# A gated-MLP kernel on one Trainium2 core: the low three bits of each weight made on ScalarE, and two weight subtractions on VectorE

## The chip, the core and the metric

The program runs on one NeuronCore of a Trainium2 chip. The core has five instruction engines, each with a queue of its own that it works off in order: TensorE (PE in the profile; its weight loads are PEld), VectorE (DVE), ScalarE (ACT), GpSimd (POOL) and SyncE (SP), which here only issues DMAs. An instruction that waits for another engine holds up everything behind it in its own queue. The metric is the device time of one execution in microseconds (us), from several timed runs. A profiled execution gives the trace; its span runs from the first to the last instruction.

## The reference, cut to what matters

An mLSTM attention over 768 steps feeds two MLPs. The arithmetic wanted is that of float32, and the weights arrive as float64.

```python
C = f_stab * C + i_stab * einsum('bhd,bhe->bhde', vt, kt)      # 768 steps, 2 x 8 heads, head size 40
n = f_stab * n + i_stab * kt
y[t] = sigmoid(o_gate[t]) * (C @ qt) / maximum(abs(n @ qt), 1)
x = y as 1536 tokens x 320
x = ((x @ w_a) * (x @ w_b)) @ w_out                            # hidden size 1536
h = x @ w_in                                                   # hidden size 2048
return (h * sigmoid(h)) @ w_out2                               # 1536 x 320
```

## The kernel before

**Attention.** The 768 steps are cut into 6 chunks of 128 for each of 2 batches: 12 units, u0 to u11. For a unit, TensorE makes the scores (L348), VectorE builds a matrix of decay factors by a running scan (L328, 128x1024) and multiplies the scores by it (L355), TensorE forms the values (L361) and the carried part (L371) and updates the state (L381), and VectorE and GpSimd finish the unit (L419 to L435). The unit is then transposed on TensorE (`px`, L451) and stored as a high and a low part in a ring of six slots (`xring`).

**MLPs.** Products are kept near float32 by splitting every factor into a high part that the fast matmul format holds and a low part, the rest after subtracting the high part. `first_layer` (L472, tile `h`) multiplies a block of two or three units by the 128 hidden columns of tile j; the first MLP does it twice, ScalarE copies one result (`a`, L505) and VectorE multiplies the two into `g` (L511). In the second MLP ScalarE applies Silu instead (L516). `split_g` splits `g`: ScalarE casts the high part (L487) and GpSimd subtracts (L196). `second_layer` (L481 to L483) accumulates into `acc`. The first MLP has 12 weight tiles, the second 16.

**Weight preparation.** Each weight is a float64, seen as two 32-bit words: `raw[..., 0]` is the low word, `raw[..., 1]` the high word. `narrowed` builds the float32 `c` (tiles `cvt`): ScalarE scales the high word so that its bits, shifted left by three, are those of the float32 (L189); VectorE shifts left by three (L190) and then takes the top three bits of the low word and ORs them in (L191). After it, ScalarE casts the high part into the weight tile `w_j`, and the subtraction `rest` (L196, a helper with one line for all callers) makes the low part. In the first MLP a weight tile comes in two pieces: part 0 of 512 elements per partition ("w3.a" in the order list), part 1 of 448 ("w3.b"). Of part 1 the first 128 columns are handled in two halves of 64 partitions: ScalarE casts a half (L213), GpSimd subtracts into a small tile `tl`, and a DMA on SP carries it to the other 64 partitions of `w_j` (L215). In the second MLP a tile is one piece of 704.

**Order.** A list written out by hand (`ORDER`) names all attention, weight and MLP steps up to the last block of the first MLP; a scheduler then places each engine's instructions by that list, by priorities and by its own estimate of when each is ready. So a changed instruction can move others. Buffers: four `raw` tiles for the first MLP and three for the second, two `cvt` tiles of each size.

The two narrow places of the code that the text needs are these, where `eng` chooses the engine of a subtraction:

```python
def rest(eng, out_, x, hi):
    return eng.tensor_tensor(out=out_, in0=x, in1=hi.bitcast(F32), op=ALU.subtract)
```

Of the kernel before, what the change touches and what calls it, by code (L numbers as in the profile page):

```python
# [8 lines left out]
F32 = mybir.dt.float32  # L9
F32R = mybir.dt.float32r  # L10
BF16 = mybir.dt.bfloat16
U32 = mybir.dt.uint32

# [51 lines left out]
ACT = mybir.ActivationFunctionType  # L67
ALU = mybir.AluOpType
# [3 lines left out]
def tile_mlstm_gated_mlps(ctx: ExitStack, tc: tile.TileContext, i_gate, f_gate, q_cols, k_cols, kvo, w1, w2,  # L72
                          out):
    nc = tc.nc
# [3 lines left out]
    P = 128  # L78
# [87 lines left out]
    raw = {}  # L166
    w1_32, w2_32 = (w.bitcast(U32).rearrange("j p (f t) -> j p f t", t=2) for w in (w1, w2))

    def load_w1(j):
        parts_ = []  # L170
        for f in (slice(0, 4 * P), slice(4 * P, 5 * P + DM)):
            t = raws.tile([P, f.stop - f.start, 2], U32, tag="raw", name=f"raw1_j{j}")
            nc.sync.dma_start(out=t, in_=w1_32[j, :, f])
# [3 lines left out]
    def load_w2(j):  # L177
        t = wp2.tile([P, 3 * P + DM, 2], U32, tag="raw2", name=f"raw2_j{j}", bufs=3)
        nc.sync.dma_start(out=t, in_=w2_32[j])
        raw[2, j] = t  # L180
# [2 lines left out]
    W = {}  # L183

    def narrowed(r, c):
        lo32, hi32 = r[:, :, 0], r[:, :, 1]
        cu = c.bitcast(U32)

        nc.scalar.activation(out=c, in_=hi32.bitcast(F32), func=ACT.Prelu, scale=2.0 ** -111, alpha=-2.0 ** 32)  # L189
        nc.vector.tensor_scalar(out=cu, in0=cu, scalar1=3, scalar2=None, op0=ALU.logical_shift_left)  # L190
        nc.vector.scalar_tensor_tensor(out=cu, in0=lo32, scalar=29, in1=cu,  # L191
                                       op0=ALU.logical_shift_right, op1=ALU.bitwise_or)
        return c

    def rest(eng, out_, x, hi):
        return eng.tensor_tensor(out=out_, in0=x, in1=hi.bitcast(F32), op=ALU.subtract)  # L196


    def split_w1(j, part):
        if (1, j) not in W:  # L200
            W[1, j] = wp.tile([P, WN], F32R, tag="w", name=f"w1_j{j}", bufs=J1)
        t, r = W[1, j], raw[1, j][part]
        if part == 0:
            c = narrowed(r, cvt.tile([P, 4 * P], F32, tag="cvt", name=f"cvt_j{j}"))
            nc.scalar.copy(out=t[:, 0:4 * P], in_=c)
            rest(nc.gpsimd, t[:, 6 * P:10 * P], c, t[:, 0:4 * P])
            return
        c = narrowed(r, cvt.tile([P, P + DM], F32, tag="cvt", name=f"cvt_j{j}"))
        tl = cvt.tile([P, P], F32R, tag="tl", name=f"tl_j{j}")
        for n in range(2):  # L210
            p, q_ = slice(n * KT, (n + 1) * KT), slice((1 - n) * KT, (2 - n) * KT)
            s_ = slice((4 + n) * P, (5 + n) * P)
            nc.scalar.copy(out=t[p, s_], in_=c[p, 0:P])  # L213
            rest(nc.gpsimd, tl[p], c[p, 0:P], t[p, s_])
            nc.sync.dma_start(out=t[q_, s_].bitcast(F32), in_=tl[p].bitcast(F32))  # L215
        nc.scalar.copy(out=t[:, 10 * P:10 * P + DM], in_=c[:, P:])
        rest(nc.gpsimd, t[:, 10 * P + DM:], c[:, P:], t[:, 10 * P:10 * P + DM])


    def split_w2(j, pool, tag, bufs):  # L220
        r = raw.pop((2, j))
        t = pool.tile([P, 5 * P + 2 * DM], F32R, tag=tag, name=f"w2_j{j}", bufs=bufs)
        c = narrowed(r, wp2.tile([P, 3 * P + DM], F32, tag="cvt2", name=f"cvt2_j{j}", bufs=2))
        nc.scalar.copy(out=t[:, 0:3 * P], in_=c[:, 0:3 * P])  # L224
        rest(nc.gpsimd, t[:, 3 * P:5 * P], c[:, 0:2 * P], t[:, 0:2 * P])
        rest(nc.gpsimd, t[KT:P, 2 * P:3 * P], c[KT:P, 2 * P:3 * P], t[KT:P, 2 * P:3 * P])
        nc.scalar.copy(out=t[:, 5 * P:5 * P + DM], in_=c[:, 3 * P:])
        rest(nc.gpsimd, t[:, 5 * P + DM:], c[:, 3 * P:], t[:, 5 * P:5 * P + DM])
        W[2, j] = t
# [358 lines left out]
    for j in range(J1):  # L588
        parts[f"lw{j}"] = lambda j=j: load_w1(j)
        parts[f"w{j}.b"] = lambda j=j: split_w1(j, 1)  # L590
        parts[f"w{j}.a"] = lambda j=j: split_w1(j, 0)
# [7 lines left out]
    for t in ORDER:  # L599
        n = t.lstrip("!")  # L600
# [112 lines left out]
```

## Time and profile before

| | us |
|---|---|
| timed runs, median of three (lowest, highest) | 496.28 (493.99, 496.87) |
| the profiled execution's own time | 493.73 |
| its span | 491.8 |
| TensorE busy | 468.7 |
| TensorE weight loads busy | 460.8 |
| GpSimd busy | 261.5 |
| ScalarE busy | 210.6 |
| VectorE busy | 199.8 |

Shares over the whole span say little here: weights are prepared in the first quarter and again around the middle, attention ends near the middle, and the last third is matmuls alone. So the profile is read by stretches of time. "Idle before, releaser" in a row is time in which the engine had nothing running, and what ended it. Matmul rows show overlapping instructions, so a mean of 300 ns does not say that one leaves every 300 ns.

### The profile page before, as it was taken

How to read it: one execution, taken by the hardware profiler on the slowest of the kernel's cores; microseconds unless marked ns; L12 is line 12 of the kernel's file. 1: busy time of each engine (PE TensorE's matmuls, PEld its weight loads, DVE VectorE, ACT ScalarE, POOL GpSimd, SP SyncE). 2: the span in 40 equal slices, each digit the busy share in tenths (PEclk: the TensorE clock that was granted, in tenths of full speed). 3: DMA queues.
4: the chain of work that ended last, by engine and by line, in shares of the span. 5: the costliest groups of instructions: out<-in, count | busy, mean ns of one | idle time of the engine just before them, and what ended most of it. 6: DMA issues, size and time to landing. Idle time of an engine off the chain costs nothing.

```text
span 491.8 us, 8440 instructions
## 1 busy us (share of the span) xinstructions
PE 468.7 (95%) x3261; PEld 460.8 (94%) x3261; DVE 199.8 (41%) x328; ACT 210.6 (43%) x479; POOL 261.5 (53%) x305
## 2 busy tenths in 40 slices
PE   7999887799999999999999999999999999999996
PEld 6988887798999999999999998899999999999996
DVE  7988989978533346523741555400100010000000
ACT  4347655563222331222645554833433453334332
POOL 5569998898432332322853877853433333343332
PEclk9888998899999999999999999999999999999999
DMA  7786857734210012105550343000010000001001
GB/s 228 218 255 205 262 174 215 210 109 131 88 55 1 14 59 58 42 1 176 176 177 1 123 171 119 0 1 1 1 41 0 1 21 21 1 0 41 1 0 40
DMA packets 25090, 42.32 MB, mean 86 GB/s; under 512 B 2156, under 2 KB 18348, under 8 KB 25052
## 3 DMA queue, kind: packets, MB, share of 16 engines
q1 hardware_dynamic: 25052, 41.80, 27.0%
q8 instruction: 25, 0.41, 0.4%
q14 instruction: 13, 0.11, 0.1%
HBM read 38.99 MB, written 2.02 MB: 83 GB/s over the span
## 4 chain that ended last, share of the span: by engine, by line
PE 67%; POOL 11%; DVE 8%; DMA 4%; issue 4%; ACT 4%; SPq 1%; ACTq 0%; POOLq 0%; DVEq 0%
PE h L472 35%; PE acc L481 8%; PE acc L483 8%; PE acc L482 8%; POOL w_j L196 7%; PE s_u L348 3%; PE y_u L361 2%; ACT cvt_j L189 2%; POOL g L196 2%; DVE e_u L328 2%; DMA raw_j<-in_w_dram 2%; DVE cvt_j L191 1%; DVE cvt_j L190 1%; PE px_u L451 1%; PE y_u L371 1%
## 5 line engine op out<-in xcount | busy, mean ns | idle before, releaser
L472 PE MATMUL h<-xring,w_j 128*128 128x384 f32 (+1 forms) x1472 | 260.3, 319 | 6.6 <-DVE g L511 4.2
L472 PEld LDWEIGHTS h<-xring,w_j 128*128 128x128 f32 x1472 | 229.9, 190 | 9.1 <-DVE g L511 5.1
L196 POOL TENSOR_TENSOR g<-g,g 128x384 fp32r<-128x384 f32 (+1 forms) x124 | 119.1, 961 | 185.5 <-ACT g L487 184.5
L487 ACT CAST g<-g 128x384 fp32r<-128x384 f32 (+1 forms) x124 | 59.8, 482 | 110.4 <-DVE g L511 71.8
L481 PE MATMUL acc<-w_j,g 128*128 128x320 f32 x336 | 102.4, 314 | 0.6 <-ACT g L487 0.6
L482 PE MATMUL acc<-w_j,g 128*128 128x320 f32 x336 | 101.0, 309 | 0.0
L483 PE MATMUL acc<-w_j,g 128*128 128x320 f32 x336 | 77.0, 313 | 1.2 <-POOL g L196 1.2
L196 POOL TENSOR_TENSOR w_j<-cvt_j,w_j 128x320 fp32r<-128x320 f32 (+2 forms) x72 | 69.7, 969 | 6.5 <-ACT w_j L224 3.0
L481 PEld LDWEIGHTS acc<-w_j,g 128*128 128x128 f32 x336 | 63.5, 189 | 1.4 <-ACT g L487 1.2
L482 PEld LDWEIGHTS acc<-w_j,g 128*128 128x128 f32 x336 | 63.5, 189 | 0.0
L483 PEld LDWEIGHTS acc<-w_j,g 128*128 128x128 f32 x336 | 56.7, 188 | 2.4 <-POOL g L196 2.4
L516 ACT ACTIVATE g<-h 128x384 f32<-128x384 f32 x64 | 31.6, 493 | 59.9 <-PE h L472 54.2
L511 DVE TENSOR_TENSOR g<-a,h 128x256 f32<-128x256 f32 (+1 forms) x60 | 28.1, 468 | 54.0 <-PE h L472 53.7
L196 DVE TENSOR_TENSOR xring<-px_u,xring 128x384 fp32r<-128x384 f32 x24 | 12.4, 548 | 85.6 <-PE h L472 82.0
L191 DVE SCALAR_TENSOR_TENSOR cvt_j<-raw_j,cvt_j 128x704 uint32<-128x704 uint32 (+2 forms) x40 | 44.7, 1118 | 0.9
L505 ACT ACTIVATE a<-h 128x256 f32<-128x256 f32 (+1 forms) x60 | 25.5, 424 | 39.1 <-PE h L472 39.1
L189 ACT ACTIVATE cvt_j<-raw_j 128x704 f32<-128x704 f32 (+2 forms) x40 | 28.9, 725 | 28.5 <-POOL w_j L196 27.0
L190 DVE TENSOR_SCALAR cvt_j<-cvt_j 128x704 uint32<-128x704 uint32 (+2 forms) x40 | 24.9, 627 | 30.1 <-ACT cvt_j L189 30.1
L348 PE MATMUL s_u<-qT_u,kz 120*128 120x128 f32 x192 | 30.9, 304 | 0.6 <-DVE y_u L419 0.6
L348 PEld LDWEIGHTS s_u<-qT_u,kz 120*128 120x128 f32 x192 | 27.4, 213 | 0.8 <-DVE y_u L419 0.8
L361 PEld LDWEIGHTS y_u<-vx_u,e_u 128*128 128x128 f32 x192 | 25.5, 197 | 1.7 <-DVE e_u L355 1.5
L361 PE MATMUL y_u<-vx_u,e_u 128*128 128x41 f32 x192 | 26.1, 274 | 0.9 <-DVE e_u L355 0.9
(83 smaller groups left out, 355.2 us busy)
## 6 DMA issues: line engine op xcount, KB each, us to landing
raw_j<-in_w_dram SPq DMA_DIRECT2D x16, 704.0 KB, 4.0
raw_j<-in_w_dram SPq DMA_DIRECT2D x12, 512.0 KB
kvo_u<-in_kvo_dram SPq DMA_DIRECT2D x12, 480.0 KB, 4.0
raw_j<-in_w_dram SPq DMA_DIRECT2D x12, 448.0 KB, 4.4
e_u<-fsd SPq DMA_DIRECT2D x10, 512.0 KB
qT_u<-in_q_cols_dram SPq DMA_DIRECT2D x12, 180.0 KB, 3.5
kz<-in_k_cols_dram SPq DMA_DIRECT2D x36, 60.0 KB
out_dram<-osb SPq DMA_DIRECT2D x12, 160.0 KB, 1.8
```

What stands on the lines that cost most here:

```text
L189: nc.scalar.activation(out=c, in_=hi32.bitcast(F32), func=ACT.Prelu, scale=2.0 ** -111, alpha=-2.0 ** 32)
L190: nc.vector.tensor_scalar(out=cu, in0=cu, scalar1=3, scalar2=None, op0=ALU.logical_shift_left)
L191: nc.vector.scalar_tensor_tensor(out=cu, in0=lo32, scalar=29, in1=cu, op0=ALU.logical_shift_right, op1=ALU.bitwise_or)
L196: return eng.tensor_tensor(out=out_, in0=x, in1=hi.bitcast(F32), op=ALU.subtract)
L348: nc.tensor.matmul(out=s[:, i], lhsT=kz[u % 2][:, j, g], rhs=un["q", u][:, g], start=True, stop=True)
L361: nc.tensor.matmul(out=T["y1"][:, h], lhsT=un["e", u][:, h], rhs=T["v"][:, h], start=True, stop=True)
L472: nc.tensor.matmul(out=po, lhsT=w[:, wi * P:(wi + 1) * P], rhs=xt[:, :, xi], start=(n == 0), stop=(n == len(pairs) - 1))
L481: nc.tensor.matmul(out=o, lhsT=hi, rhs=w[:, off:off + DM], start=first, stop=False)
L482: nc.tensor.matmul(out=o, lhsT=hi, rhs=w[:, off + DM:off + 2 * DM], start=False, stop=False)
L483: nc.tensor.matmul(out=o, lhsT=lo, rhs=w[:, off:off + DM], start=False, stop=last)
L487: nc.scalar.copy(out=t[:, 0], in_=g)
L516: nc.scalar.activation(out=g, in_=ph, func=ACT.Silu, scale=1 / WS)
```

## The change

Three things are done differently in the preparation of a weight. The shift of 128x448, 128x512 or 128x704 words on VectorE (L190) goes. A second ScalarE instruction is new: it reads the top byte of each low word, multiplies by 1/32, subtracts 15.5/32 and writes the rounded result, the top three bits, as a 32-bit integer over the front of the `raw` tile (`low`). The one VectorE instruction that is left now shifts `c` left by three and ORs `low` in. And the two subtractions into `tl` of each tile of the first MLP run on VectorE, not on GpSimd; the other subtractions stay.

```diff
     def narrowed(r, c):
-        lo32, hi32 = r[:, :, 0], r[:, :, 1]
-        cu = c.bitcast(U32)
-
-        nc.scalar.activation(out=c, in_=hi32.bitcast(F32), func=ACT.Prelu, scale=2.0 ** -111, alpha=-2.0 ** 32)
-        nc.vector.tensor_scalar(out=cu, in0=cu, scalar1=3, scalar2=None, op0=ALU.logical_shift_left)
-        nc.vector.scalar_tensor_tensor(out=cu, in0=lo32, scalar=29, in1=cu,
-                                       op0=ALU.logical_shift_right, op1=ALU.bitwise_or)
+        n = c.shape[-1]
+        cu, low = c.bitcast(U32), r.rearrange("p f t -> p (f t)")[:, 0:n]
+
+        nc.scalar.activation(out=c, in_=r[:, :, 1].bitcast(F32), func=ACT.Prelu, scale=2.0 ** -111,
+                             alpha=-2.0 ** 32)
+
+        nc.scalar.activation(out=low, in_=r.bitcast(U8)[:, :, 3], func=ACT.Copy, scale=2.0 ** -5,
+                             bias=-15.5 / 32)
+        nc.vector.scalar_tensor_tensor(out=cu, in0=cu, scalar=3, in1=low,
+                                       op0=ALU.logical_shift_left, op1=ALU.bitwise_or)
         return c
...
             nc.scalar.copy(out=t[p, s_], in_=c[p, 0:P])
-            rest(nc.gpsimd, tl[p], c[p, 0:P], t[p, s_])
+            rest(nc.vector, tl[p], c[p, 0:P], t[p, s_])
             nc.sync.dma_start(out=t[q_, s_].bitcast(F32), in_=tl[p].bitcast(F32))
```

In the changed file the lines up to `narrowed` stand one lower and those from `rest` on four lower: L191 becomes L195, L196 becomes L200, L328 becomes L332, L511 becomes L515; L193 is the new ScalarE instruction. The scheduler orders all engines anew.

VectorE at the first weight tile (`cvt_j0`), with the scan of unit u1 (`e_u1`) among its steps; before:

```order
L190 TENSOR_SCALAR cvt_j0_427<-cvt_j0_427 128x448
L190 TENSOR_SCALAR cvt_j0_440<-cvt_j0_440 128x512
L328 SCALAR_TENSOR_TENSOR e_u1_332<-fb_u1_345,ident8_93 128x512
L191 SCALAR_TENSOR_TENSOR cvt_j0_427<-raw1_j0_381,cvt_j0_427 128x448
L191 SCALAR_TENSOR_TENSOR cvt_j0_440<-raw1_j0_379,cvt_j0_440 128x512
```

and after:

```order
L195 SCALAR_TENSOR_TENSOR cvt_j0_427<-cvt_j0_427,raw1_j0_381 128x448
L195 SCALAR_TENSOR_TENSOR cvt_j0_440<-cvt_j0_440,raw1_j0_379 128x512
L332 SCALAR_TENSOR_TENSOR e_u1_332<-fb_u1_345,ident8_93 128x512
L200 TENSOR_TENSOR tl_j0_431<-cvt_j0_427,w1_j0_426 64x128 x2
L431 SCALAR_TENSOR_TENSOR dn_u0_402<-y_u0_393 128x8
```

The scan now stands behind both OR instructions, and the two `tl` subtractions behind the scan.

VectorE at weight tile 4, around a product `g` of the first MLP (`x_u2` finishes unit u2, `e_u3` weights the scores of unit u3, `e_u4` is the scan of u4); before:

```order
L432 TENSOR_TENSOR x_u2_750<-kvo_u2_446,dn_u2_746 128x320
L435 COPY x_u2_750<-x_u2_750 128x64
L511 TENSOR_TENSOR g_646<-a_589,h_647 128x256
L190 TENSOR_SCALAR cvt_j4_720<-cvt_j4_720 128x448
L191 SCALAR_TENSOR_TENSOR cvt_j4_720<-raw1_j4_621,cvt_j4_720 128x448
L355 TENSOR_TENSOR e_u3_480<-s_u3_689,e_u3_480 128x512
L328 SCALAR_TENSOR_TENSOR e_u4_814<-e_u4_814,ident8_93 128x1024
```

and after:

```order
L436 TENSOR_TENSOR x_u2_750<-kvo_u2_446,dn_u2_746 128x320
L439 COPY x_u2_750<-x_u2_750 128x64
L195 SCALAR_TENSOR_TENSOR cvt_j4_720<-cvt_j4_720,raw1_j4_621 128x448
L515 TENSOR_TENSOR g_646<-a_589,h_647 128x256
L200 TENSOR_TENSOR tl_j4_724<-cvt_j4_720,w1_j4_719 64x128 x2
L359 TENSOR_TENSOR e_u3_480<-s_u3_689,e_u3_480 128x512
L332 SCALAR_TENSOR_TENSOR e_u4_814<-e_u4_814,ident8_93 128x1024
```

The OR of tile 4 now stands ahead of the product `g`, not behind it, and the `tl` pair stands between the product and the weighting of unit u3's scores.

ScalarE where the second MLP begins (`w2_j14` and `w2_j15` are its last two weight tiles; the table load belongs to Silu); before:

```order
L189 ACTIVATE cvt2_j15_3632<-raw2_j15_3629 128x704
L224 CAST w2_j14_3619<-cvt2_j14_3620 128x384
L227 CAST w2_j14_3619<-cvt2_j14_3620 128x320
L516 ACT_TABLE_LOAD
L516 ACTIVATE g_3641<-h_3645 128x384
L487 CAST g2_3655<-g_3641 128x384
L516 ACTIVATE g_3658<-h_3659 128x384
```

and after:

```order
L190 ACTIVATE cvt2_j15_3632<-raw2_j15_3629 128x704
L228 CAST w2_j14_3619<-cvt2_j14_3620 128x384
L231 CAST w2_j14_3619<-cvt2_j14_3620 128x320
L193 ACTIVATE raw2_j15_3629<-raw2_j15_3629 128x704
L520 ACT_TABLE_LOAD
L520 ACTIVATE g_3641<-h_3645 128x384
L520 ACTIVATE g_3658<-h_3659 128x384
L491 CAST g2_3655<-g_3641 128x384
```

The new instruction for the last weight tile stands directly ahead of the table load and the first Silu, and the cast of the first `g` moved behind the second Silu.

## Rows read from the trace of the kernel before

**Rows 1.** Busy time by stretch: stretch, length, engines busy (instructions), granted clock, DMA share, GB/s.

```profile
0.00:34.00 34.00, 28.95 (x282) 27.68 (x283) 28.81 (x45) 14.06 (x30) 19.01 (x39) 0.91 0.76 233
34.00:125.00 91.00, 79.10 (x594) 75.86 (x593) 77.58 (x117) 50.93 (x132) 82.89 (x92) 0.94 0.60 184
125.00:225.00 100.00, 100.00 (x776) 99.95 (x775) 44.27 (x101) 25.74 (x65) 31.98 (x43) 1.00 0.14 40
225.00:315.00 90.00, 88.12 (x531) 85.18 (x530) 46.20 (x62) 49.12 (x100) 59.90 (x65) 1.00 0.38 128
315.00:492.00 177.00, 172.50 (x1084) 172.14 (x1084) 2.97 (x6) 70.77 (x153) 67.69 (x68) 1.00 0.04 12
```

**Rows 2.** TensorE's largest waits, 34 to 125 us: us in total, times, longest.

```profile
PE h L472 <- DVE g L511: 4.2, 3, 2.7
```

**Rows 3.** TensorE's longest wait in that stretch, and the busy row behind it.

```profile
82.81 2.08 PE L472 MATMUL h<-xring,w_j 128*128 128x256 f32 x8 [2.71 <-DVE g L511]
84.00:96.00 12.00, 10.96 (x70) 10.69 (x68) 11.39 (x16) 7.44 (x21) 10.56 (x12) 0.78 0.81 236
```

**Rows 4.** The chain that ended last, from 34 to 125 us, by line.

```profile
by line: PE h L472 12.4%; issue 10.6%; PE s_u L348 8.1%; DVE cvt_j L191 6.7%; DVE cvt_j L190 6.0%; DVE e_u L328 5.2%; POOL tl_j L196 4.9%; POOL w_j L196 4.7%; DMA w_j<-tl_j 3.5%; PE y_u L371 3.1%; PE y_u L361 3.0%; DVE x_u L432 2.4%; DMA kz
```

**Rows 5.** Groups by line and shape, 34 to 125 us: busy us, mean ns, idle before.

```profile
L196 POOL TENSOR_TENSOR tl_j<-cvt_j,w_j 64x128 fp32r<-64x128 f32 x20 | 15.8, 792 | 3.3 <-ACT w_j L213 2.5
...
L190 DVE TENSOR_SCALAR cvt_j<-cvt_j 128x448 uint32<-128x448 uint32 x10 | 8.0, 805 | 5.0 <-ACT cvt_j L189 5.0
...
L189 ACT ACTIVATE cvt_j<-raw_j 128x512 f32<-128x512 f32 x10 | 6.7, 675 | 2.4 <-POOL w_j L196 2.2
L189 ACT ACTIVATE cvt_j<-raw_j 128x448 f32<-128x448 f32 x10 | 6.1, 613 | 6.0 <-POOL w_j L196 5.8
...
L190 DVE TENSOR_SCALAR cvt_j<-cvt_j 128x512 uint32<-128x512 uint32 x10 | 5.6, 559 | 1.7 <-ACT cvt_j L189 1.6
```

**Rows 6.** Shortest, median and longest time of an instruction (ns), by tile, whole run.

```profile
L190 DVE TENSOR_SCALAR cvt_j<-cvt_j x40: 357/527/1522, 16.9 to 312.5; 128x704 uint32<-128x704 uint32 x16, 128x448 uint32<-128x448 uint32 x12, 128x512 uint32<-128x512 uint32 x12
...
L196 POOL TENSOR_TENSOR tl_j<-cvt_j,w_j x24: 447/609/2487, 19.8 to 111.4; 64x128 fp32r<-64x128 f32 x24
```

**Rows 7.** GpSimd in order of time, 73.5 to 83 us: start, us.

```profile
74.51 1.28 POOL L196 TENSOR_TENSOR w_j<-cvt_j,w_j 128x512 fp32r<-128x512 f32 x1
...
78.72 2.41 POOL L196 TENSOR_TENSOR tl_j<-cvt_j,w_j 64x128 fp32r<-64x128 f32 x1
```

**Rows 8.** VectorE in the same stretch.

```profile
74.52 1.52 DVE L190 TENSOR_SCALAR cvt_j<-cvt_j 128x448 uint32<-128x448 uint32 x1 [1.35 <-ACT cvt_j L189]
...
78.60 2.28 DVE L328 TENSOR_TENSOR_SCAN e_u<-e_u,ident 128x1024 f32<-128x1024 f32 x1
```

**Rows 9.** VectorE, two SBUF inputs, 128 elements in each partition: count, mean ns.

```profile
L254 DVE TENSOR_TENSOR scratch<-scratch 16x128 f32<-16x128 f32 x1 | 0.3, 254 | 0.0
```

**Rows 10.** VectorE at the first weight tile, in order of time.

```profile
16.89 0.69 DVE L190 TENSOR_SCALAR cvt_j<-cvt_j 128x448 uint32<-128x448 uint32 x2
17.50 1.20 DVE L328 TENSOR_TENSOR_SCAN e_u<-fb_u,ident 128x512 f32<-128x512 f32 x1
18.64 1.73 DVE L191 SCALAR_TENSOR_TENSOR cvt_j<-raw_j,cvt_j 128x448 uint32<-128x448 uint32 x2
```

**Rows 11.** DMA issue on SP right after it.

```profile
19.82 0.39 SPq L163 DMA_DIRECT2D e_u<-fsd  x1
```

**Rows 12.** ScalarE from 285 to 316 us: one cast among the weights, and the entry to Silu.

```profile
300.60 0.51 ACT L487 CAST g<-g 128x384 fp32r<-128x384 f32 x1 [1.18 <-DVE g L511]
...
313.20 1.28 ACT L516 ACT_TABLE_LOAD   x1
```

**Rows 13.** TensorE at the same two places.

```profile
302.76 0.31 PE L481 MATMUL acc<-w_j,g 128*128 128x320 f32 x1
...
315.04 1.66 PE L472 MATMUL h<-xring,w_j 128*128 128x384 f32 x8 [0.80 <-ACT g L516]
```

**Rows 14.** ScalarE's scaling of a second-MLP weight, 225 to 315 us, by line and shape.

```profile
L189 ACT ACTIVATE cvt_j<-raw_j 128x704 f32<-128x704 f32 x16 | 13.6, 849 | 16.6 <-POOL w_j L196 16.6
```

More of the change, by code (lines that the diff above doesn't have):

```diff
@@ L12 @@
 U32 = mybir.dt.uint32
+U8 = mybir.dt.uint8
 PASSES = ((0, range(0, 5)),
```

## The prediction

> **What bounds the kernel now.** I read the busy time by stretch first [rows 1]. From 125 us on TensorE is the bound: 100.00 of 100 us, then 88.12 of 90, then 172.50 of some 177. In the first 34 us its time is mostly filler matmuls and the kernel waits for gates and the first weights. What other engines can still give lies between 34 and 125 us, where attention, the first MLP and its weight preparation share all engines: TensorE is idle for 91.00 - 79.10 = 11.9 us, and its granted clock is 0.94 there, 0.06 x 91 = 5.5 us of full-speed work lost. That is a ceiling of 17.4 us for this stretch. GpSimd is the fullest there (82.89 of 91), then TensorE, then VectorE (77.58); ScalarE has 40 us free. TensorE waits mostly for VectorE's product `g` [rows 2]; after the longest such wait, 2.71 us, eight matmuls take 2.08 us, and the granted clock of the 12 us around is 0.78, between the two levels of 2.4 and 1.2 GHz [rows 3]. The chain of waits in the stretch is spread over many lines: of 91 us the shift L190 has 6.0%, or 5.5 us; the `tl` subtractions on GpSimd 4.9%, or 4.5 us; "issue", in which nothing visible is waited for, 10.6%, or 9.6 us [rows 4].
>
> Why VectorE and GpSimd are both full shows in single instructions. The shift takes 357 ns at its shortest, but a mean of 805 for 448 words in this stretch [rows 5, 6]. One took 1.52 us from 74.52 while GpSimd ran a subtraction from 74.51 to 75.79; a `tl` subtraction, 447 ns at its shortest, took 2.41 from 78.72 beside a VectorE scan from 78.60 to 80.88 [rows 6 to 8]. Two such instructions do not run side by side: one ends, then the other does its work. Removing either kind of work shortens both queues.
>
> **The shift L190 goes.** In the stretch these are 20 instructions, 8.0 + 5.6 = 13.6 us of VectorE [rows 5], of which the chain holds 5.5 us, a share of 0.40. I count -5.5.
>
> **The `tl` subtractions leave GpSimd.** 20 instructions, 15.8 us [rows 5], 4.5 us on the chain: -4.5. On VectorE each is a two-input subtraction of 128 elements; the nearest row takes 254 ns [rows 9], 20 x 0.254 = 5.1 us. With L190's share of 0.40 that puts 2.0 us on the path (ends: 0 and 5.1): +2.0. They wait for ScalarE's casts, and behind each pair on VectorE stand the weighting of scores or the next scan, for which TensorE waits; this wait is a rival below.
>
> The row pairs above show exclusion. The Trainium skill, SBUF — State Buffer (SBUF: two separate sides), calls it an exclusive lock: whichever of a GpSimd instruction and a VectorE instruction with two SBUF inputs starts first holds the shared port pair, the other waits. By that rule the moved subtraction still takes the lock, for about 0.25 us where it held it for up to 0.45, so the move alone would free at most 20 x 0.2 = 4 us of the pair; that lies under the 4.5 taken, and the sum would be 0.5 us less favourable. The trace agrees with the exclusion, with 1.52 against 0.36 us.
>
> **The "issue" part.** Where it is VectorE stuck behind GpSimd it falls with GpSimd's load, by 15.8 of 82.89, or 19%: -1.8.
>
> **The new ScalarE instruction.** The trace has no ScalarE instruction that reads bytes. The nearest rows are L189, which reads the high words at the same distance: 613 and 675 ns [rows 5], so 10 x 0.613 + 10 x 0.675 = 12.9 us in the stretch, ScalarE going from 50.9 to 63.8 of 91. What hides it is ScalarE's idle time; without that cover all 12.9 would count. L189 itself is not among the lines of the chain down to 2.4% (2.2 us), though it takes as long [rows 4, 5]; I take +2.0 (ends: 0 and 12.9).
>
> The Trainium skill, ScalarE: Activation LUTs (Rules for kernel authors), speaks against this step: add and multiply belong on VectorE, not on ScalarE. By engine time alone that would be right, 0.64 us against 0.36 per instruction, some 40 x 0.28 = 11 us for the worse; the stretch decides against the rule as far as ScalarE has idle time.
>
> The OR stays one instruction with two tensors and the same counts, so it costs what it did. Sum of the stretch: -5.5 - 4.5 - 1.8 + 2.0 + 2.0 = **-7.8 us**. Its ends: -17.3, if nothing is added to the chain and the clock loss of 5.5 goes too; +8.0, if 5.1 and 12.9 count in full against the 10.0 removed.
>
> **The start.** The scan of unit u1 ended at 17.50 + 1.20 = 18.70 [rows 10]. Now the OR pair stands ahead of it and no shift does: 16.89 + 1.73 + 1.20 = 19.82. The `tl` pair follows, to 20.3, where before the OR pair ended, at 20.4. So VectorE is on time after that, but SP's load of `e_u` for u2, issued at 19.82 [rows 11], now has the first `tl` transfer ahead of it in SP's queue: some 20.1 plus half a microsecond of issue. I count **+0.8** (ends: -0.7, the shifts saved, and +1.5).
>
> **The second preparation, 225 to 315 us.** 16 new instructions of 849 ns [rows 14] are 13.6 us on a ScalarE that is idle for 41 of 90 [rows 1]; TensorE can gain no more than its 1.9 us of idle time. Eleven of the 16 stand right ahead of a copy `a` or a cast of `g`. A cast that ended at 301.11 was used at 302.76 [rows 12, 13], a slack of 1.65 us against 0.85: hidden, 0. One place is not: the last one stands directly ahead of the Silu table load, behind which TensorE already waits 0.80 us at 315.04. There I count **+0.85**. (Ends: -1.9 and +13.6.)
>
> **Sum.** -7.8 + 0.8 + 0.85 = -6.15. The profiled execution took 493.73, so 487.6 on its basis; it is 2.55 us under the median of the timed runs, 496.28. I forecast for the median: **490.1 us**, 1.2% faster. About 1% is what a measurement of this kernel can tell from no change.
>
> **Rivals.**
> - *The wait moves to VectorE: no change.* GpSimd was idle 3.3 us ahead of `tl` for the casts [rows 5]; on VectorE that stands ahead of what TensorE waits for, and all 5.1 us of the subtractions count, 3.1 more. -6.15 + 3.3 + 3.1 = +0.25, or 496.5. For it: VectorE's `g` already leads TensorE's waits. Against: an OR of the other piece or a scan mostly stands between the first OR and its `tl` pair. 0.22.
> - *Much better.* With the shared time relieved, TensorE's idle and its low clock both go for the most part: half way from -6.15 to -17.3 + 1.65, -10.9, or 485.4. For it: one wait of 2.71 us is followed by a 0.78 clock. Against: so many lines share the chain that the next is close. 0.10.
> - *The new instruction doesn't do what it says.* If reading single bytes 8 apart, or writing integers, takes twice as long, ScalarE has 50.9 + 25.8 = 76.7 us of 91, as full as VectorE, and at VectorE's share of 0.40 it puts 10.3 us on the path, not 2.0. -6.15 + 8.3 = +2.2, or 498.4. For it: no row has such an operand. Against: L189 with its stride costs nearly what a plain cast does. 0.08.
> - *Slower: ScalarE's order in the second preparation.* There ScalarE waits for GpSimd to free `cvt` (16.6 us [rows 14]), and what stands behind it, casts of `g` included, waits too. If 0.85 us on top exceeds the slack of 1.65 us that is left (the point from which it decides), each of the 16 tiles delays TensorE: 16 x 0.85 = 13.6, less the 0.85 counted: -6.15 + 12.75 = +6.6, or 502.9. For it: TensorE idles 1.9 us there already. Against: the slack seen is twice the delay. 0.12.
>
> **Chances and range.** The forecast has 0.48. Its own spread, some 2.2 us from the shares taken for the chain, puts about 0.7 of that beyond 1% faster (under 491.3), which is 0.34; with the better case and a remnant of the first rival 0.45. Slower by over 1% (over 501.2) is most of the last rival and the tail of the third, 0.13; within 1% is left with 0.42. The range 483 to 500 holds the forecast, the first three rivals' times and the ends of the start; it leaves out the slow rival and the far tails, about 0.2.
>
> **What would show it.** Between 34 and 125 us: GpSimd's busy time down from 82.9 by some 15; VectorE's by 8 or more, its OR closer to its shortest time; ScalarE's up by some 13, the new instruction at 0.61 to 0.85 us; TensorE's idle time down from 11.9 to about 6, and its granted clock at or over 0.94. The end of the mixed stretch would come some 7 us earlier, and TensorE's wait at the entry to Silu grow to 1.6 us. I am wrong if the new instruction takes over 1 us, if TensorE's waits for `g` or for the scores stay at their size with `tl` or the casts L213 named ahead of them on VectorE, or if its idle time from 225 to 315 us grows by several microseconds.

## The result, and the profile after

The changed kernel is slower: 503.01 us median (499.96 to 505.81) against 495.13 (493.97 to 496.87), a ratio of 1.015, interval 1.010 to 1.020. Timed once more beside other kernels it gave 502.03 and 1.010 (1.005 to 1.015). The forecast was 490.1 in a range of 483 to 500, so it missed, and on the wrong side. The profiled execution took 505.81 us, its span 504.1. Executions more than 1.5% above the fastest of the same kernel ran at a lower mean clock than that one, and the ratios and the means over several executions below leave them out, while the medians hold all.

Busy time by stretch in the changed kernel, with the columns of [rows 1]:

```profile
0.00:34.00 34.00, 30.50 (x252) 29.25 (x252) 25.20 (x42) 14.52 (x29) 12.77 (x34) 0.80 0.64 209
34.00:125.00 91.00, 76.88 (x563) 74.29 (x562) 74.29 (x115) 60.74 (x153) 61.42 (x68) 0.89 0.63 191
125.00:225.00 100.00, 97.54 (x744) 97.15 (x743) 43.03 (x95) 24.91 (x64) 32.95 (x45) 0.97 0.14 41
225.00:315.00 90.00, 89.28 (x554) 87.82 (x553) 30.12 (x46) 51.25 (x102) 50.71 (x56) 1.00 0.37 121
315.00:504.00 189.00, 183.93 (x1157) 183.35 (x1155) 8.06 (x14) 82.12 (x175) 77.54 (x79) 1.00 0.05 15
```

GpSimd is 21 us less busy between 34 and 125 us, as meant, and ScalarE 10 us more. But TensorE did not fill up: it has 14.1 idle us there instead of 11.9, its granted clock is 0.89 instead of 0.94, and the loss goes on behind 125 us, where TensorE had no idle time before and now has 2.5 us, at 0.97. The loss lies in the mixed stretch and the start; from 225 us on the kernel is no worse than before.

TensorE's largest waits, 34 to 125 us, answering to [rows 2]: us in total, times, longest.

```profile
PE h L476 <- DVE g L515: 5.7, 4, 2.8
PE pgb L294 <- DVE isg L289: 3.0, 1, 3.0
PE y_u L365 <- DVE e_u L359: 2.8, 2, 2.5
PE px_u L455 <- DVE x_u L436: 2.2, 1, 2.2
```

All four name VectorE, whose load in the stretch went down from 77.58 to 74.29 us. How it comes to be late all the same shows at single waits. The longest is for the copy `isg`; VectorE ahead of it, then TensorE:

```profile
34.45 2.29 DVE L332 TENSOR_TENSOR_SCAN e_u<-e_u,ident 128x1024 f32<-128x1024 f32 x1 [0.72 <-DMA e_u<-fsd]
36.65 1.63 DVE L200 TENSOR_TENSOR tl_j<-cvt_j,w_j 64x128 fp32r<-64x128 f32 x2
38.31 0.33 DVE L289 COPY isg<-pg 128x160 f32<-128x160 f32 x1
```

```profile
38.69 1.69 PE L294 MATMUL pgb<-scratch 16*120 16x6 f32 x12 [3.00 <-DVE isg L289]
```

The `tl` pair takes 1.63 us right ahead of the copy. It stands as close ahead of a product `g` for which TensorE waits 2.24 us:

```profile
103.85 1.11 DVE L200 TENSOR_TENSOR tl_j<-cvt_j,w_j 64x128 fp32r<-64x128 f32 x2 [0.36 <-ACT w_j L217]
105.00 0.42 DVE L515 TENSOR_TENSOR g<-a,h 128x256 f32<-128x256 f32 x1
```

```profile
105.47 1.21 PE L476 MATMUL h<-xring,w_j 128*128 128x256 f32 x8 [2.24 <-DVE g L515]
```

The longest wait for `g` has no `tl` pair ahead of it. VectorE in order of time ahead of 120 us:

```profile
115.66 1.20 DVE L436 TENSOR_TENSOR x_u<-kvo_u,dn_u 128x320 f32<-128x320 f32 x1
116.85 2.29 DVE L332 TENSOR_TENSOR_SCAN e_u<-e_u,ident 128x1024 f32<-128x1024 f32 x1
119.06 0.79 DVE L439 COPY x_u<-x_u 128x64 f32<-128x64 f32 x1
119.76 0.41 DVE L515 TENSOR_TENSOR g<-a,h 128x256 f32<-128x256 f32 x1
```

TensorE at the same place, and the 12 us around it by busy time and clock:

```profile
120.22 1.22 PE L476 MATMUL h<-xring,w_j 128*128 128x256 f32 x8 [2.84 <-DVE g L515]
```

```profile
120.00:132.00 12.00, 11.78 (x71) 11.73 (x72) 5.66 (x15) 3.15 (x8) 8.01 (x11) 0.72 0.16 45
```

Here the product `g` stands behind a scan of 2.29 us and a copy of 0.79; TensorE waits 2.84 us, and then runs part of the following 12 us at the lower of its two clock levels, as it did before at 82.8 us [rows 3]. So such a wait can be paid for twice, though not every one is: behind one of 2.79 us at 97.75 in before the clock stayed at 1.00. Over the timed executions the mean granted clock was 0.980 before (43 executions, mean span 493.5 us) and 0.969 after (9, 500.1). Span times what is missing to 1 is the most that the clock can have cost, since a low clock costs nothing where TensorE waits anyway: 9.8 us before and 15.5 after, a difference of 5.7 beside one of 6.6 in span.

VectorE's weight instructions in the stretch, answering to [rows 5]: busy us, mean ns, idle before.

```profile
L200 DVE TENSOR_TENSOR tl_j<-cvt_j,w_j 64x128 fp32r<-64x128 f32 x22 | 12.5, 567 | 0.7 <-ACT w_j L217 0.4
L195 DVE SCALAR_TENSOR_TENSOR cvt_j<-cvt_j,raw_j 128x448 uint32<-128x448 uint32 x10 | 9.5, 951 | 2.0 <-POOL w_j L200 1.1 <-issue 0.6 <-ACT raw_j L193 0.2
L195 DVE SCALAR_TENSOR_TENSOR cvt_j<-cvt_j,raw_j 128x512 uint32<-128x512 uint32 x10 | 8.1, 808 | 1.3 <-POOL w_j L200 1.1 <-issue 0.2
```

And the new ScalarE instruction (L193) beside the scaling (L190):

```profile
L193 ACT ACTIVATE raw_j<-raw_j 128x512 uint32<-128x512 uint8 x10 | 6.7, 673 | 0.0
L190 ACT ACTIVATE cvt_j<-raw_j 128x512 f32<-128x512 f32 x10 | 6.7, 671 | 1.6 <-POOL w_j L200 1.6
L193 ACT ACTIVATE raw_j<-raw_j 128x448 uint32<-128x448 uint8 x10 | 6.2, 618 | 0.2
```

The shift's 13.6 us left VectorE, and 12.5 us of `tl` came. VectorE hardly waited at `tl` for ScalarE (0.4 us), so the rival in which the casts hold it up is out. Shortest, median and longest of a `tl` subtraction, to be read against GpSimd's 447/609/2487 [rows 6]:

```profile
L200 DVE TENSOR_TENSOR tl_j<-cvt_j,w_j x24: 258/328/1325, 20.5 to 120.4; 64x128 fp32r<-64x128 f32 x24
```

What parts the short ones from the long is GpSimd. Of the 22 between 34 and 125 us, nine ran while no GpSimd instruction did, and each took 271 to 290 ns, 284 in the mean. The other thirteen overlapped with a GpSimd instruction and took 763 ns in the mean. In a second profile of the same kernel (e4_again below) the two means are 283 and 744.

### The profile page after: what moved, and what is told of

The parts are those of the page before. It is cut to its first block, busy times and chain, and to the rows that moved or that the text cites. A ratio compares the mean times of both kernels' runs of the same rounds, so it can differ in the third digit from the quotient of the medians.

```text
span 504.1 us, 8458 instructions
## 1 busy us (share of the span) xinstructions
PE 478.1 (95%) x3261; PEld 471.9 (94%) x3261; DVE 180.7 (36%) x312; ACT 233.5 (46%) x519; POOL 235.4 (47%) x281
## 5 line engine op out<-in xcount | busy, mean ns | idle before, releaser
L476 PE MATMUL h<-xring,w_j 128*128 128x384 f32 (+1 forms) x1472 | 264.5, 322 | 10.3 <-DVE g L515 8.2
L476 PEld LDWEIGHTS h<-xring,w_j 128*128 128x128 f32 x1472 | 233.0, 192 | 13.0 <-DVE g L515 9.4
L200 POOL TENSOR_TENSOR g<-g,g 128x384 fp32r<-128x384 f32 (+1 forms) x124 | 119.3, 962 | 192.7 <-ACT g L491 192.6
L200 POOL TENSOR_TENSOR w_j<-cvt_j,w_j 128x320 fp32r<-128x320 f32 (+2 forms) x72 | 68.3, 948 | 26.8 <-ACT w_j L220 11.0
L515 DVE TENSOR_TENSOR g<-a,h 128x256 f32<-128x256 f32 (+1 forms) x60 | 28.1, 470 | 66.8 <-PE h L476 57.8
L195 DVE SCALAR_TENSOR_TENSOR cvt_j<-cvt_j,raw_j 128x704 uint32<-128x704 uint32 (+2 forms) x40 | 36.3, 911 | 36.0 <-POOL w_j L200 15.1
L200 DVE TENSOR_TENSOR xring<-px_u,xring 128x384 fp32r<-128x384 f32 x24 | 12.4, 549 | 84.6 <-ACT xring L458 84.5
L190 ACT ACTIVATE cvt_j<-raw_j 128x704 f32<-128x704 f32 (+2 forms) x40 | 28.9, 724 | 13.4 <-POOL w_j L200 10.5
L352 PE MATMUL s_u<-qT_u,kz 120*128 120x128 f32 x192 | 32.7, 314 | 0.0
L365 PEld LDWEIGHTS y_u<-vx_u,e_u 128*128 128x128 f32 x192 | 29.2, 219 | 3.4 <-DVE e_u L359 2.7
L365 PE MATMUL y_u<-vx_u,e_u 128*128 128x41 f32 x192 | 29.6, 292 | 2.8 <-DVE e_u L359 2.8
L352 PEld LDWEIGHTS s_u<-qT_u,kz 120*128 120x128 f32 x192 | 29.2, 224 | 0.1
L193 ACT ACTIVATE raw_j<-raw_j 128x704 uint32<-128x704 uint8 (+2 forms) x40 | 28.8, 722 | 0.3
```

Source lines behind the costliest of these rows:

```text
L190: nc.scalar.activation(out=c, in_=r[:, :, 1].bitcast(F32), func=ACT.Prelu, scale=2.0 ** -111, alpha=-2.0 ** 32)
L193: nc.scalar.activation(out=low, in_=r.bitcast(U8)[:, :, 3], func=ACT.Copy, scale=2.0 ** -5, bias=-15.5 / 32)
L195: nc.vector.scalar_tensor_tensor(out=cu, in0=cu, scalar=3, in1=low, op0=ALU.logical_shift_left, op1=ALU.bitwise_or)
L352: nc.tensor.matmul(out=s[:, i], lhsT=kz[u % 2][:, j, g], rhs=un["q", u][:, g], start=True, stop=True)
L365: nc.tensor.matmul(out=T["y1"][:, h], lhsT=un["e", u][:, h], rhs=T["v"][:, h], start=True, stop=True)
L476: nc.tensor.matmul(out=po, lhsT=w[:, wi * P:(wi + 1) * P], rhs=xt[:, :, xi], start=(n == 0), stop=(n == len(pairs) - 1))
```

## The experiments

Three theories stood at first. **A**: what counts is the order in which the instructions come to stand; the program's order is worked out anew for each kernel, and the change gets a worse one. **B**: the `tl` pair on VectorE holds up what TensorE waits for. **C**: the new ScalarE instruction costs by itself. Each kernel is compared with runs of the kernel before on the same chip (medians 495.1 to 495.9); a ratio is turned into microseconds with 495.6.

| kernel | what it is | median us | ratio to before (95%) | us by the ratio |
|---|---|---|---|---|
| e1_new_low_only | low bits on ScalarE, `tl` on GpSimd | 497.37 | 1.002 (0.999 to 1.006) | +1.1 |
| e2_tl_only | `tl` on VectorE alone | 505.88 | 1.017 (1.008 to 1.025) | +8.3 |
| e3_start_old | change from the third slice on | 499.53 | 1.006 (1.001 to 1.010) | +2.8 |
| e_w2_only | low bits on ScalarE, second weights alone | 495.01 | 0.999 (0.995 to 1.003) | -0.5 |
| e4_again | the change once more | 502.03 | 1.010 (1.005 to 1.015) | +5.1 |
| n149_before | before, one filler less | 498.08 | 1.007 (1.004 to 1.010) | +3.4 |
| n151_before | before, one filler more | 499.36 | 1.005 (1.001 to 1.008) | +2.2 |
| e9_no_low | before without shift and or | 484.07 | 0.978 (0.973 to 0.982) | -11.0 |
| pin_low | first half, before's order | 500.25 | 1.008 (1.005 to 1.012) | +4.2 |
| pin_tl | second half, before's order | 504.40 | 1.014 (1.008 to 1.019) | +6.8 |
| pin_after | whole change, before's order | 511.31 | 1.028 (1.023 to 1.034) | +14.0 |
| pin_rev | before's instructions, after's order | 505.03 | 1.017 (1.011 to 1.022) | +8.2 |
| q_low | as pin_low, second preparation free | 492.42 | 0.994 (0.991 to 0.997) | -3.0 |
| q_noshift | before without the shift, its order | 490.20 | 0.986 (0.981 to 0.992) | -6.9 |
| q_notl | before without `tl` on GpSimd, its order | 500.35 | 1.008 (1.004 to 1.012) | +3.9 |
| q_dummy | before and a pair on VectorE, its order | 515.05 | 1.039 (1.034 to 1.044) | +19.5 |
| q_notl2 | as q_notl, no buffer held | 497.28 | 0.998 (0.994 to 1.003) | -0.9 |
| q_dummy2 | as q_dummy, no buffer held, 20 instructions | 505.36 | 1.022 (1.016 to 1.028) | +10.7 |

**The halves apart.** In e1_new_low_only and e2_tl_only one half each:

```diff
 e1_new_low_only, against after
-            rest(nc.vector, tl[p], c[p, 0:P], t[p, s_])
+            rest(nc.gpsimd, tl[p], c[p, 0:P], t[p, s_])
 e2_tl_only, against before
-            rest(nc.gpsimd, tl[p], c[p, 0:P], t[p, s_])
+            rest(nc.vector, tl[p], c[p, 0:P], t[p, s_])
```

> The change without its second half: ScalarE makes the low bits and VectorE shifts and ors in one step, but the two 64x128 subtractions into tl stay on GpSimd. Theory A (the loss lies in the order at the start: the program's instructions on TensorE, SP and VectorE stand otherwise before the first h, and first h comes 8 us later): the order ahead of the first h is again another one than before's, so the time follows the first h, by about as much as it is later than 32.4 us; if it is at 32 to 34, the time is 490 to 496, if at 38 to 41, 500 to 504. Theory B (the tl pair on VectorE stands ahead of the scan, the isg copy and the g products that TensorE waits for): 488 to 494, with first h near 33. Theory C (the new ScalarE instruction lengthens the chain from raw to weight and keeps ScalarE's order busy): 500 to 504, as slow as the whole change.

> Only the second half of the change: the two 64x128 subtractions into tl go to VectorE, the low word is still shifted and or'ed by VectorE in two steps as before. Theory A: the time follows the first h, as in the run beside it; what stands before the first h is here nearer to before's order, so 494 to 500. Theory B: 501 to 508, since VectorE here has the tl pair and the shift too. Theory C: 493 to 497.

In e3_start_old the first two slices are made as before (`j > 1` decides), in e_w2_only all of the first weights.

> The whole change, but the first two weight slices (j0 and j1, those that are prepared before the first h) are made as before: shift and or on VectorE, tl on GpSimd. Everything ahead of the first h then stands in before's order. Theory A: first h at 32 to 34 us and 488 to 495. Theory B: 20 of 24 tl instructions are still on VectorE, so 499 to 503. Theory C: 20 of 24 new ScalarE instructions of the first weights are still there, 499 to 503.

> The new way of making the low word only for the second weights, the first weights as before, tl on GpSimd. All queues stand as before up to the second preparation. Theories A and B: 493 to 496, as before, by at most 1 us better (TensorE's idle time between 225 and 315 us was 1.9 us before and 0.7 after). Theory C: 496 to 498, if the ScalarE instruction costs wherever it stands.

The second half alone is as slow as the whole change or slower; the first half alone costs little or nothing, and in the second weights nothing. That speaks for B and against C, though e1_new_low_only, with 497.37 us, lies between the ranges of all three. It doesn't dispose of A, since each of these kernels also has an order of its own, and e3_start_old lies between.

**Is the early fall of the clock the change's doing?** In the changed kernel TensorE fell to the lower clock near 12 us: the 35 filler matmuls there took 3.91 us, in before 2.13.

> The changed kernel once more, unedited, for a second profile and for more times. In the first profile TensorE had the half clock from 12.4 to 26 us, and a kernel whose order up to 225 us is that of before showed the same fall there (12 to 24 us at 0.51) with a time of 500.6 against its median of 495.0. If that early fall is a draw of each execution and not the change's doing, this profile may well show the clock held there, and the time is then 497 to 500; the median stays at 501 to 505 all the same if the rest of the loss lies behind the start. If the early fall belongs to the change, it is there again.

Busy time from 12 to 24 us in the changed kernel, then in e3_start_old (before's instructions and order up to there), then in e1_new_low_only (new instructions):

```profile
12.00:24.00 12.00, 12.00 (x75) 11.35 (x76) 8.38 (x11) 4.74 (x12) 4.07 (x5) 0.52 0.60 212
```

```profile
12.00:24.00 12.00, 12.00 (x74) 11.36 (x74) 8.53 (x11) 3.15 (x9) 4.39 (x6) 0.50 0.51 178
```

```profile
12.00:24.00 12.00, 12.00 (x124) 11.42 (x121) 10.79 (x16) 7.37 (x15) 5.97 (x8) 0.86 0.78 252
```

The fall is there without the change and can be missing with part of it, so it differs from execution to execution: the first `h` at 40.31 us in the first profile, 7.9 us later than before's 32.42, overstates the loss. In e4_again the fall came again (0.50), so its profile didn't settle how the change runs without it, and whether the change makes the fall more likely stays open; its median and its best time, 497.86 against 493.4 for before, suggest that the rest of the loss stays.

**Order alone.** One filler matmul less or more, some 50 ns at the start, and nothing else:

```diff
-    WARM = 150
+    WARM = 149
```

> The kernel before with 149 filler matmuls at the start instead of 150: some 50 ns of filler less, no other edit; the order on every engine comes out another way from about 20 us on. Theory A (what counts is the order that the program gets, and before's is a good draw of it): 497 to 503, slower by 2 to 7, with TensorE waiting at other places and longer at the half clock. Theories B and C (the instructions that the change adds): 494 to 497, the same as before.

> The kernel before with 151 fillers instead of 150, a second draw of the order. Theory A: 496 to 503, and not by need the same as with 149. Theories B and C: 494 to 497.

Both are slower, by 2 to 3 us, without any instruction of the change. So before's order is better than two others that it could have had, and an edit that makes the order come out anew may pay about this much. That is A, but as a part of the loss.

**Is VectorE's weight work on the path at all?**

> The kernel before with VectorE's shift and or left out altogether (the weights are then wrong: only ScalarE's scaled high word is left), the tl subtractions on GpSimd as before. It takes some 60 us of work from VectorE, half of it between 34 and 125 us, and no work is added anywhere. If that work is on the path that sets the end (as my prediction had it, at 5.5 us for the shift alone): 480 to 488. If the mixed stretch is bound by TensorE's own instructions and by the chain of the attention chunks: 490 to 496.

It is: -11.0 us, in an order of its own.

**The same order for all.** Here the order of the kernel before is written out, each instruction behind the one that stands ahead of it on its engine, by an edge that sets the order of issue and no wait (the lists are left out):

```diff
+    traced = [i for i in nc.cur_bb.bb.instructions if type(i).__name__.startswith("Inst")]
+    for row in PINNED:
+        row = [traced[int(n)] for n in row.split()]
+        for first, second in zip(row, row[1:]):
+            tc.add_manual_dep(second, first.name, ...)
```

> The whole change, with the order of the kernel before written out on every engine: each instruction issues where it stands in before, each new ScalarE instruction right behind the scaling of its tile, the shift left out, the tl pair on VectorE right behind the second or of its slice. Theory A (the loss is the order that the change gets, not the instructions): 486 to 493, faster than before by about what my prediction summed for the stretch 34 to 125 us. Theory B (the tl pair on VectorE costs by itself, wherever order puts the rest): 499 to 505. Theory C (the new ScalarE instruction costs): 497 to 505.

> Only the first half of the change (low bits on ScalarE, shift and or in one step, tl on GpSimd), in the order of the kernel before, written out. Theory A: 487 to 493. Theory B: 488 to 494, and clearly faster than the whole change in the same order. Theory C: 496 to 500.

> Only the second half (tl pair on VectorE behind the second or of its slice, shift and or as before), in the order of the kernel before, written out. Theory A: 493 to 498, about as before. Theory B: 502 to 507, as slow as the same edit was in its own order (505.9). Theory C: 494 to 497.

> The instructions of the kernel before in the order of the changed kernel, written out: the shift right ahead of its or, the tl pair on GpSimd right ahead of the 128x320 subtraction of its slice. Theory A: 499 to 506, slower than before by as much as the changed kernel is or more, since the shift comes on top. Theories B and C: 493 to 498, as before, since no instruction of the change is in it.

A as sole cause falls: in before's order the change is slower still, by 14.0 us, more than any of the three theories expected, and both halves cost, 4.2 and 6.8; pin_low's 500.25 us is about what C expected. Nor is after's order simply bad: with before's instructions it gives 505. An order fits the instructions that it was worked out for. But where pin_low and pin_after lost time tells a second thing. TensorE's waits in pin_after, 225 to 335 us, and the busy row from 225 to 315:

```profile
PE acc L674 <- ACT g L680: 3.8, 4, 1.0
PE acc L676 <- POOL g L389: 1.7, 6, 0.3
PE h L665 <- ACT a L698: 1.2, 4, 0.4
```

```profile
225.00:315.00 90.00, 86.20 (x530) 83.45 (x529) 27.92 (x44) 49.16 (x94) 45.02 (x52) 1.00 0.32 113
```

ScalarE there, in order of time: the new instruction (L382) stands ahead of the cast of `g` (L680) that TensorE waits for.

```profile
305.86 0.84 ACT L379 ACTIVATE cvt_j<-raw_j 128x704 f32<-128x704 f32 x1 [1.95 <-POOL w_j L389]
306.72 0.83 ACT L382 ACTIVATE raw_j<-raw_j 128x704 uint32<-128x704 uint8 x1
307.45 0.50 ACT L680 CAST g<-g 128x384 fp32r<-128x384 f32 x1
```

That is the mechanism of the rival "Slower: ScalarE's order in the second preparation". It needs this order: in the changed kernel's own, TensorE is busy 89.28 us of the stretch. q_low below, pin_low with the second preparation left free, is 7.2 us faster than pin_low, which speaks against C in the mixed stretch.

**One term at a time, in before's order.** q_low leaves the second preparation free. The other edits take away or add one thing:

```diff
 q_noshift
-        nc.vector.tensor_scalar(out=cu, in0=cu, scalar1=3, scalar2=None, op0=ALU.logical_shift_left)
 q_notl; in q_notl2 in_=t[p, s_].bitcast(F32)
-        tl = cvt.tile([P, P], F32R, tag="tl", name=f"tl_j{j}")
...
-            rest(nc.gpsimd, tl[p], c[p, 0:P], t[p, s_])
-            nc.sync.dma_start(out=t[q_, s_].bitcast(F32), in_=tl[p].bitcast(F32))
+            nc.sync.dma_start(out=t[q_, s_].bitcast(F32), in_=c[p, 0:P])
 q_dummy2; in q_dummy for every j, with out= a raw tile
+        if j > 1:
+            for n in range(2):
+                p = slice(n * KT, (n + 1) * KT)
+                nc.vector.tensor_tensor(out=idb[p], in0=ident[p], in1=ident[p], op=ALU.subtract)
```

> The first half of the change (low bits on ScalarE, tl on GpSimd), the order of the kernel before written out for everything up to the second preparation, the order of the second preparation and of what follows left to the program. If pin_low lost its time in the second preparation, where the order written out put each new ScalarE instruction ahead of work that TensorE waited for (TensorE was busy 84.9 us there instead of 88 to 89), and gained 2 to 3 us ahead of it: 491 to 495. If the new ScalarE instruction costs in the mixed stretch too: 497 to 501, as pin_low.

> The kernel before in its own order, written out, with VectorE's shift left out and nothing in its place (the weights are then wrong). By my prediction's term the shift is worth 5.5 us: 488 to 491. If VectorE's time isn't what the mixed stretch ends on: 494 to 497. If its whole time (some 15 us between 34 and 125) is on the path, more: 480 to 486.

> The kernel before in its own order, written out, with a pair of 64x128 subtractions of constants added on VectorE behind the second or of each slice; their results go into a raw tile that is already read and nobody waits for them; tl stays on GpSimd. If the price of the second half of the change is VectorE's time (13 us of it between 34 and 125, and what stands behind it): 500 to 505, as pin_tl. If it is a wait or a release that hangs on tl itself (the ScalarE copies ahead of it, the buffer of the unsplit weights that it holds): 495 to 498. By my prediction's term for tl on VectorE (+2): 497 to 499.

> The kernel before in its own order, written out, with GpSimd's tl subtractions left out and nothing in their place; the transfer that moves tl takes the unsplit columns instead (the weights are then wrong). By my prediction's term this frees 4.5 us: 489 to 492. If what GpSimd does there isn't what TensorE or VectorE wait for: 494 to 497.

q_dummy and q_notl each held a buffer longer, which added waits (ScalarE 10.1 us for chunk loads in the one, 1.2 in before; 12.0 us behind the transfer in the other, none in before), so neither prices its term; the next two are cleaner.

> The kernel before in its own order, written out, with a pair of 64x128 subtractions of constants added on VectorE behind the second or of each slice from the third on (20 of them; 13 to 14 us between 34 and 125); they write into the constant that the fillers at the start read, which nobody uses by then, so that no buffer is held. If VectorE's time is the price of the second half: 503 to 510. If the 515 of the run before came from the raw tile that it held: 496 to 500. My prediction's term (+2): 497 to 498.

> The kernel before in its own order, written out, without GpSimd's tl subtractions; the transfer takes the columns that ScalarE has already copied (the weights are then wrong), so that no buffer is held longer. By my prediction's term (-4.5): 489 to 492. If GpSimd's time isn't on the path: 494 to 497. If it is worth as much as pin_tl and the added pair together say (pin_tl cost 8.8 with GpSimd relieved): 485 to 489.

Before with nothing but its order written out was not timed. The traces stand in for it: in q_dummy2 every engine has before's instructions in before's order, with as many waits, and the 20 new ones between them. For q_notl2 the trace says less: its profiled execution took 502.96 us, far from the median of 497.28, and ScalarE waited 5.8 us for chunk loads in it.

Of q_dummy2, the stretch from 34 to 125 us by busy time, the added pair by shape, and the chain that ended last:

```profile
34.00:125.00 91.00, 75.67 (x501) 72.42 (x501) 81.49 (x128) 48.77 (x128) 74.12 (x85) 0.83 0.59 179
```

```profile
L410 DVE TENSOR_TENSOR idb<-ident 64x128 bf16<-64x128 f32 x20 | 11.8, 592 | 0.1
```

```profile
by line: issue 14.9%; DVE cvt_j L380 12.2%; DVE idb L410 8.6%; PE s_u L541 6.5%; DVE cvt_j L379 6.4%; PE y_u L554 6.0%; PE h L665 5.3%; DVE e_u L521 4.0%; DVE e_u L548 3.7%; ACT cvt_j L378 3.6%; DVE dn_u L622 3.5%; POOL w_j L385 3.1%; DVE x
```

Twenty subtractions that nobody waits for take 11.8 us, are on the chain with 8.6% of 91, or 7.8 us, and cost 10.7 us of the whole. The granted clock goes from 0.94 to 0.83. They write bf16 where `tl` is float32, but take as long (592 ns in the mean, against 567). Taking VectorE's shift away lets TensorE do more in the stretch; in q_noshift, then in q_low:

```profile
34.00:125.00 91.00, 81.61 (x615) 79.95 (x616) 64.61 (x99) 50.91 (x134) 82.26 (x95) 0.92 0.60 181
```

```profile
34.00:125.00 91.00, 82.25 (x608) 79.56 (x608) 63.59 (x98) 62.06 (x153) 80.25 (x94) 0.92 0.62 183
```

TensorE gets through 615 and 608 matmuls in these 91 us, against 594 before, 563 in the changed kernel and 501 in q_dummy2.

## Why the prediction was wrong

- **What bounds the kernel.** Right: VectorE's work in the mixed stretch is on the path. Wrong was the weight between the two full queues: GpSimd, the fullest, had little to give.
- **"The shift L190 goes": -5.5.** Right. In before's order its removal alone gave -6.9 (-9.7 to -4.2).
- **"The `tl` subtractions leave GpSimd": -4.5, and "issue": -1.8.** Wrong as far as the runs go. GpSimd without them, nothing put elsewhere: -0.9 (-3.2 to +1.3). They held 4.9% of the chain [rows 4], but taking them off it freed little. This term is the least certain: pin_tl, in which GpSimd is relieved too, cost 3.9 us less than q_dummy2, in which it is not, with intervals of about 3 us to either side of both. The 6.3 us that the two terms sum to lie outside the first figure's interval.
- **"On VectorE ... +2.0 (ends: 0 and 5.1)": the step that failed.** Twenty subtractions of the same size cost +10.7 (7.7 to 13.7). The duration was taken from an instruction in the start, 254 ns [rows 9], at 7.16 us, while GpSimd ran nothing; alone a `tl` subtraction takes about that long (284 ns), but beside a GpSimd instruction it took 763, the mean is 567, and 12.5 us and not 5.1 came onto VectorE. The prediction had read from [rows 7, 8] that such instructions do not run side by side, and counted this as a gain of the move; it did not count that the moved instruction would wait for GpSimd in its turn. (Of its two row pairs only the one beside the scan has a VectorE instruction with two SBUF inputs, as in the rule that it quotes; the shift has one.) Then 0.40 of the time was to be on the path, and the bound stopped at the whole of it; measured was 10.7 for 11.8, nearly all of it. Part of that is the clock: in the mean of its executions q_dummy2 loses up to 19.5 us to it, before on the same chip up to 10.6. The bound from above left the clock out, though [rows 3] showed it.
- **"The new ScalarE instruction": +2.0.** Right in duration (forecast 613 and 675 ns, measured 618 and 673). In size it agrees as far as the runs can tell: q_low against q_noshift differs by it alone up to the second preparation, 6.9 - 3.0 = 3.9 by the ratios, whose intervals are 3 to 6 us wide. The Trainium skill, ScalarE: Activation LUTs (Rules for kernel authors), would leave multiply and add to VectorE; on a stretch where VectorE's shift cost 6.9 and the ScalarE instruction 3.9, the measurement decides against it.
- **"The OR stays ... what it did".** Nearly: 951 ns for 448 words and 808 for 512, against 965 and 976 before.
- **"The start": +0.8.** Open. The first `h` came at 40.31 and 42.96 us in the two profiles, and part of it is the early fall of the clock, which also comes without the change. Leaving the first two slices as before gave +2.8 where the change gave +5.1 and +7.4, but that also takes 4 of 24 `tl` instructions away.
- **"The second preparation": +0.85.** About right: TensorE's wait at the entry to Silu was 1.2 us (0.80 before), its busy time there 89.28 us instead of 88.12.
- **Not in the prediction: the order.** Its sum compares instructions as if the rest stood still. One filler less or more cost 3.4 and 2.2 us, and the first half of the change gives +1.1 in its own order and -3.0 in before's.

Put together in before's order: -6.9 (shift) + 3.9 (ScalarE) - 0.9 (GpSimd) + 10.7 (VectorE) = +6.8. The first two are q_low's -3.0 again. The last two, +9.8 for moving the pair, can be held against runs in the same order that move it: pin_after less pin_low, 14.0 - 4.2 = +9.8, and pin_tl, +6.8, which still has the shift. For the change in its own order +5.1 and +7.4 were measured; that this agrees with +6.8 may be partly chance, as orders alone differ by some 3 us. Of the rivals, "The wait moves to VectorE" had the right place and the wrong price: it let the subtractions count with 5.1 us and kept GpSimd's gain. The wait for ScalarE's casts, from which it started, did not come (0.4 us).

The runs point to a better kernel than both: the first half alone, in before's order up to the second preparation (q_low), 492.42 us, 0.994 (0.991 to 0.997).

## What to carry to other kernels

Price what is moved onto a nearly full engine at its duration while the other engines work, not at its shortest, and count the lower clock that can follow a late product; a dummy instruction of the same shape that nobody waits for measures that price directly. An engine that is fuller is not for that the one to relieve: take the work away, put nothing in its place, and see. Where a program orders its own instructions, measure an edit that changes nothing but the order before believing a difference of one per cent, and write the order out to compare instructions alone.

## What the runs showed of the hardware

- The same fillers in the same place ran at either clock. With them the stretch from 12 to 24 us was granted 0.50 to 0.52 or 0.86. Over the 43 executions of the kernel before that are counted above, the time went from 493.4 to 498.9 us, with mean clocks from 0.986 down to 0.969.
- A 64x128 subtraction on VectorE took 284 ns in the mean of nine during which GpSimd ran nothing, and 763 in the mean of thirteen that overlapped with a GpSimd instruction; GpSimd was busy 61.42 of 91 us. The Trainium skill, SBUF — State Buffer (Who interferes with whom), says that a VectorE instruction with two SBUF inputs contends with a GpSimd instruction that reads SBUF; the durations agree, and they give the price: about half a microsecond for each overlap.
- ScalarE reading single bytes eight apart and writing 32-bit integers (618 ns for 448 and 673 for 512) cost what the scaling of 32-bit words at that distance did (616 and 671).
